# A recurrence with a feed-forward block on one core: the order of 6028 steps and the PSUM pairs of 499 rooms exchanged

## The chip, the cores and the metric

The kernel runs on one core of a Trainium2 chip. Its time is the device time in microseconds of one execution. The median of three runs of the kernel before is 1084.03 us (1081.16 to 1093.83).

## What is computed

The reference runs a state recurrence over 768 time steps for 4 batches of 8 heads, each with a 40 × 40 state, and feeds its output, as 3072 tokens of 320 numbers, to a feed-forward block with a gate:

```python
def _attn_ref(r, k, v, w, a, b):                # each (4, 8, 768, 40), float32
    ...
    for t in range(S):
        ...
        y[:, :, t] = np.einsum('bhd,bhde->bhe', rt, state)
        Sa = np.einsum('bhde,bhe->bhd', state, at)
        state_decay = state * wt[:, :, None, :] - np.einsum('bhd,bhe->bhde', Sa, bt)
        state = state_decay + np.einsum('bhd,bhe->bhde', vt, kt)
    return y

def _moe_ref(x, w_gate, w_val, w_out, rms_g):   # x (3072, 320), d_ff = 1536
    rms = np.sqrt(np.mean(x * x, axis=-1, keepdims=True) + 1e-06)
    xn = x / rms * rms_g
    g = xn @ w_gate
    silu = g * (1.0 / (1.0 + np.exp(-g)))
    val = xn @ w_val
    return silu * val @ w_out
```

The three weight matrices and the norm's gain come as given by the set-up; the matrices arrive as 64-bit floats and are narrowed to 32 bits on the chip.

## The kernel before

Time is cut into 24 chunks of 32 steps, and the recurrence inside a chunk is made into matrix products. For each chunk there are three stages, and for each two chunks a fourth:

- `front(c)` loads w, a (`wan`), k, b (`kbn`), v (`VU`) and every second w (`wn`) of the chunk, by DMAs that POOL issues (SP and ACT for chunk 0), turns them by TensorE transposes (`turned`, "turn"), and makes, by "gramk" matmuls, the products of keys with decayed a. Level by level (1, 2, 4, 8, 16 steps) DVE masks these products into the triangular matrix `LT` (`where`, a predicated copy) and forms the decayed `K`, `Ab` and `KN`; ACT copies. LT goes to DRAM (`sB`) and comes back in another layout as `M`.
- `early_inverse(c)` (chunks 0 to 3) or `inverse(c)` (the others) inverts that matrix by pairs of small DVE steps `tmp` and `Yi` (or `M`), 31 pairs for a late chunk. The result goes to DRAM (`sY`) and comes back into `LT` (or, for chunks 0 to 3, `M`) by DMAs of SP.
- `main(c)` carries the state: "state" and "lower" matmuls (`LT` with `VU`), ACT's `Xs`, a second "lower" with the inverse, a copy into `VU`, "update", a new state `ST`; then the outputs: "score" matmuls, DVE's eight masked copies `As`, one "level" matmul group for each of the five levels, and DVE's `y` steps that put them together. Then comes the norm: transposes ("turn4"), a square with sum on ACT, a `ts` on DVE, a power on POOL, a scaling on ACT, transposes ("turn3") and `xg`, the input of the feed-forward block.
- `feed(g)` (12 groups of two chunks) runs six double slices of the hidden layer: two loads `wf` from the narrowed weights `sW`, "h64" and "h" matmuls into PSUM, ACT's `sg` (SiLU), DVE's `hT`, "out" matmuls into `po`; in the end a copy `o` and the store.
- `narrow`, 24 times in the first group, loads half a slice of raw weights, makes 32-bit floats of it on ACT and DVE (`ex`), and stores it into `sW`.

None of these issues its instructions at once. `Plan.add` (L282) records each as a step with its engine and its dependences. L446 makes DVE's steps, L466, L469 and L472 ACT's, L475, L478 and L481 POOL's, L485 a DMA's issue, L488 a matmul and L491 a transpose (so nearly all rows of a profile name these helpers). A step on PE is a group of matmuls, such as the 64 of one "gramk".

`Plan.issue` (L324) then issues all 6028 steps in one written order, `ORDER` (L33 to L228), each word of which is the place of a step counted from the first step in program order that has not been issued yet. Each engine's queue is the part of this order that belongs to it, and an engine takes its queue in order: a step that waits holds up all behind it on its engine. The steps are 905 on PE, 2858 on DVE, 1024 on ACT, 545 on POOL and 696 on SP, which issues DMAs only. A word "-" stands for a filler: one 128 × 128 matmul of `ident` into an unread part of `po` (L1017). There are 151 of them.

Every PSUM result but `po` is a room: a request for one of three pairs of PSUM banks (`ps0` to `ps2`). `PAIRS` (L230 to L236) gives one digit for each of the 499 rooms, the pair that it takes. A pair holds one room at a time (`held` in `Plan.issue`): the first step that writes a room waits until the last step that reads the pair's former room is done.

The chunk and the place of a step inside its stage name it below: "front 14" is the stage `front` of chunk 14, "inverse 6" the inverse of chunk 6.

## Time and profile before

| what | us |
|---|---|
| runs: median (lowest, highest) | 1084.03 (1081.16, 1093.83) |
| span of the profiled execution | 1078.2 |
| ACT busy | 462.2 |
| POOL busy | 309.0 |

| stretch, us from the start | PE busy | DVE busy | ACT busy | POOL busy | granted PE clock |
|---|---|---|---|---|---|
| 0 to 27 | 18.09 | 20.81 | 16.70 | 25.66 | 1.00 |
| 27 to 54 | 21.60 | 22.86 | 22.07 | 19.33 | 0.75 |
| 54 to 81 | 17.66 | 21.68 | 12.64 | 4.66 | 0.79 |
| 81 to 108 | 21.45 | 19.53 | 15.56 | 11.13 | 0.83 |
| 108 to 162 | 48.40 | 41.98 | 35.28 | 14.99 | 1.00 |
| 162 to 216 | 51.88 | 48.50 | 37.01 | 18.36 | 1.00 |
| 216 to 324 | 105.73 | 78.63 | 48.15 | 31.38 | 1.00 |
| 324 to 432 | 104.59 | 92.56 | 41.18 | 29.77 | 1.00 |
| 432 to 540 | 104.01 | 87.86 | 44.97 | 32.20 | 0.98 |
| 540 to 648 | 105.38 | 93.39 | 43.64 | 35.74 | 1.00 |
| 648 to 756 | 103.92 | 89.88 | 41.82 | 27.42 | 0.98 |
| 756 to 864 | 102.12 | 86.64 | 42.15 | 32.11 | 1.00 |
| 864 to 972 | 105.41 | 92.43 | 43.49 | 25.13 | 1.00 |
| 972 to 1078.2 | 99.96 | 37.48 | 17.54 | 1.11 | 0.99 to 1.00 |

Until about 162 us the weights are narrowed and the first chunks come in, and fillers stand between PE's steps. From then on a stretch of some 82 us holds two chunks of the recurrence and one group of the feed-forward block. Some groups of the profile, with the mean time of one instruction:

```profile
L488 PE MATMUL ps<-xg,wf 128*128 128x256 f32 (+1 forms) x1728 | 355.2, 392 | 4.7 <-DVE xg L446 1.1
L488 PE MATMUL po<-wf,hT 128*128 128x320 f32 x576 | 180.1, 445 | 0.1
L446 DVE TENSOR_TENSOR tmp<-Yi,M 128x60 f32<-128x60 f32 (+24 forms) x620 | 129.5, 209 | 19.7 <-DMA M<-sB 6.9
L446 DVE TENSOR_TENSOR hT<-ps,sg 128x256 f32<-128x256 f32 x144 | 59.0, 419 | 62.4 <-ACT sg L466 55.9
L446 DVE TENSOR_TENSOR As<-ps,msi 128x256 f32<-128x256 f32 (+1 forms) x186 | 79.2, 475 | 18.3 <-PE ps L488 17.4
L488 PE MATMUL ps<-Ab,K 40*64 40x56 f32 x4608 | 88.0, 225 | 8.8 <-ACT K L469 3.7
```

A row is read thus: line, engine, operation, the tile written and the tiles read, count; behind the bar the busy time in us and the mean of one in ns; behind the second bar the idle time of the engine just before these instructions, and what ended most of it. A matmul instruction overlaps the next, so 64 of a "gramk" take 1.1 us and not 64 × 0.225.

### The profile page before, as it was taken

The numbers are of one execution on the slowest core, as the hardware profiler recorded it, in microseconds if no ns is written. First come the engines' busy times: TensorE is split into PE (matmuls) and PEld (weight loads), VectorE is DVE, ScalarE is ACT, GpSimd is POOL, SyncE is SP. The second block draws the span as 40 slices with busy tenths as digits, with TensorE's granted clock in tenths as the row PEclk, the third lists the DMA queues.
The fourth block names the chain that finished last, engine by engine and source line by source line (L and its number), as shares of the span: only waits on it lengthen the run. The fifth ranks groups of instructions, "written<-read, shape, count | busy, mean of one in ns | idle before, by whom it ended". The sixth has DMA issues, their size and how long they took to land. (4 is left out here: it accounts for less than half of the span.)

```text
span 1078.2 us, 53465 instructions
## 1 busy us (share of the span) xinstructions
PE 1010.2 (94%) x23406; PEld 828.3 (77%) x23406; DVE 834.2 (77%) x2861; ACT 462.2 (43%) x1043; POOL 309.0 (29%) x554
## 2 busy tenths in 40 slices
PE   6767899999999999999999999998999999999998
PEld 6766778777888787877788778887777887887776
DVE  7887879876868888887897888887788889797420
ACT  6845756643543433532443434433344344342211
POOL 9714404120532223241331331331332331200000
PEclk9778999999999999999999999999999999999999
DMA  9965448766564364574465654665545553744242
GB/s 180 196 155 123 73 106 220 213 127 177 124 142 122 99 150 116 144 145 120 96 152 133 146 126 112 142 142 123 126 106 110 134 150 90 162 109 123 77 140 86
DMA packets 172456, 143.34 MB, mean 133 GB/s; under 512 B 125504, under 2 KB 143872, under 8 KB 172224
## 3 DMA queue, kind: packets, MB, share of 16 engines
q1 hardware_dynamic: 153856, 116.96, 42.4%
q0 software_dynamic: 16192, 22.64, 12.2%
q8 instruction: 184, 3.01, 1.2%
q10 hardware_dynamic: 2176, 0.33, 0.2%
q14 instruction: 48, 0.39, 0.1%
HBM read 123.86 MB, written 15.99 MB: 130 GB/s over the span
## 5 line engine op out<-in xcount | busy, mean ns | idle before, releaser
L488 PE MATMUL ps<-xg,wf 128*128 128x256 f32 (+1 forms) x1728 | 355.2, 392 | 4.7 <-DVE xg L446 1.1
L488 PEld LDWEIGHTS ps<-xg,wf 128*128 128x128 f32 (+1 forms) x1728 | 261.6, 189 | 60.4 <-issue 16.9
L488 PE MATMUL po<-wf,hT 128*128 128x320 f32 x576 | 180.1, 445 | 0.1
L446 DVE TENSOR_TENSOR tmp<-Yi,M 128x60 f32<-128x60 f32 (+24 forms) x620 | 129.5, 209 | 19.7 <-DMA M<-sB 6.9
L446 DVE TENSOR_TENSOR Yi<-Yi,tmp 128x60 f32<-128x60 f32 (+24 forms) x620 | 130.2, 210 | 12.7 <-DVE ss L446 0.2
L466 ACT ACTIVATE sg<-ps 128x256 f32<-128x256 f32 x144 | 52.4, 383 | 192.4 <-PE ps L488 182.7
L488 PEld LDWEIGHTS po<-wf,hT 128*128 128x128 f32 x576 | 102.6, 191 | 34.0 <-issue 1.7
L485 POOL DMA_DIRECT2D VU<-in_v_dram x92 | 53.6, 587 | 234.2 <-PE ps L488 157.0
L446 DVE TENSOR_TENSOR hT<-ps,sg 128x256 f32<-128x256 f32 x144 | 59.0, 419 | 62.4 <-ACT sg L466 55.9
L469 ACT COPY KN<-ps 128x640 f32<-128x640 f32 x96 | 66.2, 691 | 76.6 <-PE ps L491 27.9
L488 PEld LDWEIGHTS ps<-Ab,K 40*64 40x64 f32 x4608 | 78.3, 139 | 26.4 <-issue 8.5
L446 DVE TENSOR_TENSOR K<-K,T 128x512 f32<-128x512 f32 (+1 forms) x192 | 93.3, 495 | 4.2 <-ACT K L469 2.1
L488 PE MATMUL ps<-Ab,K 40*64 40x56 f32 x4608 | 88.0, 225 | 8.8 <-ACT K L469 3.7
L485 POOL DMA_DIRECT2D kbn<-in_b_dram x92 | 53.4, 584 | 147.9 <-PE ps L488 147.0
L446 DVE TENSOR_TENSOR As<-ps,msi 128x256 f32<-128x256 f32 (+1 forms) x186 | 79.2, 475 | 18.3 <-PE ps L488 17.4
L469 ACT COPY K<-K 128x256 f32<-128x256 f32 (+1 forms) x168 | 71.8, 443 | 41.3 <-PE ps L488 20.3
L488 PEld LDWEIGHTS ps<-As,KN 128*40 128x40 f32 x3072 | 64.6, 122 | 15.1 <-issue 9.7
L485 POOL DMA_DIRECT2D wn<-in_w_dram x92 | 51.6, 565 | 83.7 <-DVE KN L446 34.7
L485 POOL DMA_DIRECT2D kbn<-in_k_dram x92 | 53.5, 585 | 73.8 <-PE ps L488 73.5
L488 PE MATMUL ps<-As,KN 128*40 128x32 f32 x3072 | 71.1, 203 | 3.7 <-issue 2.7
L446 DVE TENSOR_TENSOR y<-y,ps 128x256 f32<-128x256 f32 x119 | 49.9, 419 | 19.7 <-PE ps L488 17.6
L446 DVE COPY_PREDICATED LT<-near,ps 128x384 f32<-128x384 uint32 (+2 forms) x72 | 52.3, 727 | 3.6 <-PE ps L488 1.9
(133 smaller groups left out, 1544.5 us busy)
## 6 DMA issues: line engine op xcount, KB each, us to landing
wf<-sW SPq DMA_DIRECT2D x144, 480.0 KB, 4.3
M<-sB SPq DMA_DIRECT2D x80, 128.0 KB, 3.8
rn<-in_r_dram SPq DMA_DIRECT2D x24, 160.0 KB, 4.5
sW<-ex SPq DMA_DIRECT2D x16, 240.0 KB, 4.3
out_dram<-o SPq DMA_DIRECT2D x48, 80.0 KB, 3.9
kbn<-in_k_dram POOLq DMA_DIRECT2D x92, 40.0 KB, 3.5
kbn<-in_b_dram POOLq DMA_DIRECT2D x92, 40.0 KB, 3.3
wan<-in_a_dram POOLq DMA_DIRECT2D x46, 80.0 KB, 4.7
```

What stands on the lines that cost most here:

```text
L446: plan.add("DVE", kind, lambda at: fn(at(o), *m(at)), [o], aps(*args))
L466: plan.add("ACT", "act", lambda at: nc.scalar.activation(at(o), at(a), f, **kw), [o] + aps(acc), [a])
L469: plan.add("ACT", "copy", lambda at: nc.scalar.copy(at(o), at(a)), [o], [a])
L485: plan.add(by, "dma", lambda at: queue.dma_start(out=o, in_=i), [o], [i])
L488: return o, lhsT, rhs, lambda at: nc.tensor.matmul(at(o), lhsT, rhs, start=start, stop=stop, skip_group_check=True)
```

## The change

The two strings `ORDER` and `PAIRS` are exchanged for others. All other lines are as before; `ORDER` is 13 lines longer, so that what is L488 before is L501 after. The same 6028 steps, 151 fillers and 499 rooms are issued. Measured by its place in its own engine's queue, a step moves by up to 11 places on PE, 132 on DVE, 41 on ACT, 59 on POOL and 56 on SP; 519, 2661, 880, 507 and 645 steps have another place than before. 54 of the 499 digits of `PAIRS` differ. Between two "gramk" groups of front 2 there are 22 fillers, where there were 9.

The strings begin and end thus:

```diff
 ORDER = """
-85 84 76 83 58 78 73 86 74 59 60 75 5 89 61 88 53 77 80 4 43 6 201 7 87 90 44 8 334 62 9 - - - - - - - - 93 10 18 79
-11 12 214 557 13 213 567 14 15 94 566 210 16 17 95 558 108 200 - - - 97 96 19 335 20 21 2 209 22 23 98 25 199 568 26
...
+74 83 557 568 84 73 75 85 78 86 77 88 76 87 58 4 214 53 44 59 43 54 5 60 38 - 93 578 89 569 558 587 567 566 335 589
+577 79 586 392 48 82 334 597 2 598 94 95 6 7 8 9 10 11 12 13 14 18 15 16 17 19 108 100 20 101 - - - - - 97 - - - 23
...
 PAIRS = """
-0120112210001221022012220120200102100112221210100202110000202212201000111120112120200021220001012222000200201102100111
-0112202000011221102122212200211202022022000011000020220020011122112120010011221011122210001020022121001222220200121010
-1220202110022021220021221222111210110202012021121000002020222101010111121000120212220000221022212022101110012021110002
-0020222022211000002121122111200011110200001202211022020010021211001202102001102012021011201220022100102222202110211111
-012000001002222222210120120
+1010212220002120120222020120201101010212221210100202110000202212201000111120112120200021220001012222000200201202100111
+0112202000011221102122212200211202022022000011000220020020011122112120010011221011122220002020022121001222220200121010
+1210202102022021220021221102111210210202012121101000000022222101011111121000120212220000221212002002101110010021210002
+0020222022211000002122122111200011110200001202211022020010021212001202102001100212021011201220022000102222202110211111
+012000001202120222210012102
 """
```

On PE, one place of the queue reads like this, before and after (chunk 17, group 7 of the feed-forward block; `vut`,`rE` are the scores, `As`,`KN` the levels, `xg`,`wf` the h matmuls):

```
before   L488 score, 64 matmuls
         L488 h of one slice of group 7, 8 matmuls
         L488 level 16, level 8, level 1, level 2, level 4, 32 matmuls each
         L488 h of the other slice, 8 matmuls
after    L501 score, 64 matmuls
         L501 level 8, 32 matmuls
         L501 h of one slice of group 7, 8 matmuls
         L501 level 16, level 1, level 4, level 2, 32 matmuls each
         L501 h of the other slice, 8 matmuls
```

## The prediction

> **What bounds the kernel now.** I read the busy times first, then TensorE's waits, then the windows by stage, then single stretches.

> ```profile
> PE 1010.2 (94%) x23406; PEld 828.3 (77%) x23406; DVE 834.2 (77%) x2861; ACT 462.2 (43%) x1043; POOL 309.0 (29%) x554
> ...
> PEclk9778999999999999999999999999999999999999
> ```

> PE is busy for 1010.2 of 1078.2 us, DVE, the next, for 834.2. PE is the bound, and time is lost where PE waits. Its share of a slice is low in the first six slices only (the prologue to 162 us: 34.8 us idle in the windows), and there the granted clock is low too. From 162 us on it has 33 us idle, and this is what ended it:

> ```profile
> PE ps L488 <- issue: 12.9, 20, 1.8
> PE ps L491 <- DMA kbn<-in_k_dram: 2.1, 3, 1.1
> PE ps L491 <- DVE T L446: 1.5, 1, 1.5
> PE ps L488 <- DMA LT<-sY: 1.3, 1, 1.3
> ```

> The columns are total, times, longest. "Issue" makes 14.4 us (12.9 in this row, 1.2 and 0.3 in two others), with no cause that the trace shows; all waits for another engine's data come to 12.3 us. So the order of before feeds PE almost without a gap, and a new order is judged by the gaps that it opens.

> **The change part by part.** No operation is added or removed: 1010.2 us of PE work, 151 fillers among it, stay. Only places change: 519 of PE's 905 steps, 2661 of DVE's 2858, 880 of ACT's 1024, 507 of POOL's 545, 645 of SP's 696 stand elsewhere in their queues, by up to 11, 132, 41, 59 and 56 places; 54 of 499 PSUM pairs differ. Engines take their queues in order, so each PE step of the new order can be held against an earlier PE step (its anchor): on the one side the PE work that now stands between the two, on the other the durations of the chain from the anchor to it, through dependences, PSUM pairs coming free, and all that its DVE, ACT, POOL or SP queue now places ahead. Where the chain is longer, PE must stand still for the difference, however far the other engines have run ahead. Held over 4 us of PE work, the old order after 162 us has six such places, 3.3 us together; the trace has waits there (1.36 worked out at 360.4 us, 1.55 seen; 0.60 and 0.65 at 641.7). That check carries the rest: the new order has some 25 places. Four of them, with the prices of before's rows:

> Chunk 17, levels. These rows are PE and, last, DVE of before:

> ```profile
> 791.65 1.06 PE L488 MATMUL ps<-rE,vut 40*64 40x32 f32 x57 [0.21 <-ACT KN L469]
> 793.11 0.31 PE L488 MATMUL ps<-rE,vut 40*64 40x32 f32 x7 [0.40 <-issue]
> 793.35 1.99 PE L488 MATMUL ps<-xg,wf 128*128 128x256 f32 x8
> 795.62 1.42 PE L488 MATMUL ps<-As,KN 128*40 128x32 f32 x64 [0.27 <-DVE As L446]
> ```
> ```profile
> 793.55 3.28 DVE L446 TENSOR_TENSOR As<-ps,msi 128x256 f32<-128x256 f32 x8 [0.77 <-PE ps L488]
> ```

> Scores come first, DVE masks them into As (eight instructions, 3.28 us), the first level needs two of these, and eight feed matmuls (1.99 us) cover that: a wait of 0.27. In the new order level 8 follows the scores directly and feed's matmuls come behind it. Its own As stands behind an As (0.41), two steps of inverse 18 (0.17 each) and four As (0.68, 0.68, 0.41, 0.41), and takes 0.42 itself; as each DVE instruction starts some 0.07 before the end of the one ahead, that is 3.0 us against no PE work: +3.0. The next level there adds 1.4.

> Chunk 5, the same pattern: one gram matmul (1.12 us) between scores and level, and a DVE queue of 3.99 us (three As and five steps of gram masks, decay, K and Ab among them) before the As: +2.9.

> Chunk 12: the first lower-triangular matmul follows the gram matmuls of front 14 directly. Its PSUM pair is freed by an hT of feed 5, and in DVE's queue two predicated copies (0.72, 0.73) that need these very gram matmuls and four inverse steps (0.22 to 0.24) stand ahead of it (0.41): +2.7. In before that matmul came at 573.71 without a wait.

> Chunk 20: its last v load stands on POOL behind the power of chunk 19's norm. From the transposes: square 0.44, sum 0.15, power 0.56, one load issue 0.65, the load until landing 2.2 to 2.4; 4.23 against 1.17 of out and 0.71 of state matmuls: +2.35.

> The others, each the same subtraction: chunk 4 0.73 and 1.97, 5 1.66 (total 7.2 at 216 to 324 us with the 2.9 above); 7 0.86, 0.95, 0.31 (2.1); 10 0.62; 12 0.84 and 13 0.17 (3.7 with the 2.7); front 16 1.71, 15 0.98 (2.7); 17 0.98, 19 2.25 (7.65 at 756 to 864 with the 4.4); 20 0.36 and 2.03, 21 0.28, 1.50, 0.92 (7.4 with the 2.35); tail 2.2. The sum is 33.7 us.

> What these edits relieve: the six old places, −3.3. Of the other 9.0 us of data waits (12.3 − 3.3) new gaps nearby will take some: bounds 0 and −9.0, I take −4.5.

> The clock. PE's granted clock halves behind some waits:

> ```profile
> 498.56 0.66 PE L488 MATMUL ps<-VU,KN 64*40 64x40 f32 x45 [1.74 <-issue]
> ```
> ```profile
> 499.84:503.26 3.42, 3.42 (x33) 2.06 (x26) 2.12 (x11) 0.69 (x1) 2.52 (x5) 0.50 0.39 64
> 752.43:755.84 3.41, 3.41 (x27) 2.35 (x28) 2.49 (x10) 0.00 (x0) 0.00 (x0) 0.50 0.52 131
> ```

> A wait of 1.74, and one of 1.81 at 751.20, were followed by 3.4 us at 0.50, which cost some 1.7 us of PE time each; waits of 1.55 (360.4) and 1.31 (526.3) were not. Eight new waits exceed 1.7. Bounds 0 and 8 × 1.7 = 13.6; I take three, +5.1, since two cases on either side fix no threshold. [...]

> The prologue. Here the end of inverse 0 sets PE's start:

> ```profile
> 75.45 0.78 PE L488 MATMUL ps<-M,LT 16*16 16x16 f32 x64 [3.96 <-DMA M<-sY]
> ```
> ```profile
> 84.16 0.41 DVE L446 TENSOR_SCALAR wf<-wf 128x480 int32<-128x480 int32 x1 [7.35 <-ACT ex L466]
> ```

> In the new order 5.5 us less DVE work (59.8 to 54.3) and 6.3 us less ACT work stand ahead of inverse 0's end, and one weight-narrowing load fewer between its two sY stores on SP, so M<-sY comes earlier and the 3.96 can go. Against that, 22 fillers instead of 9 stand between two gram steps of front 2 (13 × 0.24 to 0.43 = 3 to 6 us if they are not in a gap). Ahead of 35.3 us the same subtraction finds eight short places in before, 7.9 us, and three in the new order, 3.1, some of them counted twice: up to 4.8 us. Bounds: −14 (3.96, 4.8 and the larger part of DVE's 7.35) and +3 (fillers alone); I take −6, the wait itself and half of the 4.8, rounded down.

> The v loads on POOL, in before ahead of their reader by 25 to 64 us, come just in time now in several chunks; their landing has 2.1/3.4/7.0 as minimum, median, maximum. The chain of chunk 20 used the short end; a long one adds 3.6 there, kept for the range. SP's weight loads of feed 1 now stand ahead of inverse 5's stores, and these move by 17 us to 272, still ahead of their reader: 0, but up to 3 if they land late.

> Sum: 33.7 − 3.3 − 4.5 + 5.1 − 6 = +25.0, a span of 1103.2. The median of the runs (1084.03) is 5.8 above the profiled span, so the time is 1109.

> **The rivals.** *First, the prologue opens (not slower).* Before 162 us the clock is at half in 35.6 to 49.3, 62.9 to 69.8, 76.6 to 86.8 and 100.5 to 103.9, 34.2 us which cost up to 17.1. If inverse 0's earlier end and the moved fillers keep the clock full there, −17 and the 3.96 replace the −6, and the clock term stays 0: 33.7 − 3.3 − 4.5 − 21 = +4.9, 1089; with DVE's 7.35 as well −2.5, 1081.5. For it: fillers are moved towards the gaps. Against: in that stage PE waits in many places (issue 11.7 us, ACT's K 6.7, po's first memset 3.3), most of which stay, and the half clock begins at 35.6, long before inverse 0 ends. It decides from a prologue gain of 15 on. Chance 0.11.

> *Second, the gaps overlap with "issue".* If PE's 14.4 us of issue waits are taken up in the new gaps, and no clock stretch follows: 33.7 − 3.3 − 9.0 − 14.4 − 6 = +1.0, 1085; with half of the 14.4, 1092. For it: the cause of the issue waits is not seen. Against: they lie at other places (498.6, 751.2) than the new gaps. Chance 0.10.

> *Third, worse.* All eight clock stretches and a late v load: 25.0 + 8.5 + 3.6 = +37, 1121. For it: both waits over 1.7 in the trace halved the clock. Chance 0.16.

> *Fourth, both of the first two:* 15 less than the second, 1070. Chance 0.05. My forecast keeps 0.58.

> **How the numbers follow.** The likeliest gives 1109. Without the clock term (−5.1), with all of the old waits gone (−4.5) and the prologue at −14 (−8) it is 1091; the range begins at 1090, which takes in the upper part of the second rival, and ends just over the third, at 1123. Outside lie the first, the fourth and the rest of the second, near 0.2. One per cent, about what a measurement of this kernel can tell from no change, is 10.8 us: 1073.2 and 1094.9. Faster: the fourth, 0.05. Same: the first and the second without its overlap with the forecast, 0.21 less some 0.05 for the part of either that ends above 1094.9, so 0.16. Slower: the rest, 0.79.

> **What would show it.** Right: level in chunks 5, 17 and 21 waiting 1.5 to 3 us on DVE As; lower in chunks 12 and 19 on DVE hT; in chunk 20 on the v load; PE idle between 216 and 972 us rising from 25 to about 50; DVE busy unchanged near 834; half-clock stretches behind some of those waits; PE's M<-sY wait below 2 us. Wrong: if these steps wait less than half of what is worked out, DVE's or ACT's queue is not what releases them, and the subtraction fails; if the prologue ends over 15 us earlier, the first rival holds.

## The result and the profile after

The changed kernel takes 1237.53 us (median of 4 runs, 1231.11 to 1240.39), before 1086.53 beside it: a ratio of 1.139, 95% interval 1.133 to 1.145. The forecast was 1109, its range ended at 1123. The sign was right, the size wrong by a factor of six.

Head of the page of after, busy time and granted clock:

```profile
PE 1065.3 (86%) x23406; PEld 865.3 (70%) x23406; DVE 836.9 (68%) x2861; ACT 457.8 (37%) x1043; POOL 310.9 (25%) x554
...
PEclk9767989898898998989988998989999989989999
```

DVE's work is what it was (834.2 and 836.9 us). PE differs twice: its own work takes 55.1 us longer (1010.2 to 1065.3), and it stands idle for 173.1 us (1238.4 − 1065.3) instead of 68.0. The two make the 160.2 us of the spans. The clock line has an 8 or less in 16 of 40 slices, where before had 9 from the fifth slice on: 43 us at half clock (a granted clock of 0.5) in before ((1 − 0.980) × 2 × 1078.2), 183 us in after ((1 − 0.926) × 2 × 1238.4). The loss is not in one place: PE is 4 to 11 us late at the steps around 162 us (the orders differ there), then about 60 at 400, 100 at 670 and 160 at the end.

TensorE's longest rows of waits in after from 162 us on (total, times, longest); all data waits of before there came to 12.3 us:

```profile
PE ps L501 <- DVE y L459: 19.6, 19, 2.3
PE ps L501 <- issue: 15.9, 12, 3.1
PE ps L501 <- DVE hT L459: 14.9, 11, 2.7
PE ps L501 <- DMA VU<-in_v_dram: 13.6, 5, 6.2
PE ps L501 <- DVE As L459: 8.2, 7, 3.1
```

As, hT and the v load are the releasers that were forecast; DVE's y, the largest row, is not among them. The worked places came out as forecast. Chunk 17 in after, PE's timeline:

```profile
909.68 1.28 PE L501 MATMUL ps<-As,KN 128*40 128x32 f32 x32 [3.09 <-DVE As L459]
910.90 2.95 PE L501 MATMUL ps<-xg,wf 128*128 128x256 f32 x8
...
916.22 0.81 PE L501 MATMUL ps<-As,kbn 128*40 128x32 f32 x32 [1.64 <-DVE y L459]
```

3.09 and 1.64 against 3.0 and 1.4. The eight h matmuls behind the wait take 2.95 us where before's took 1.99: the granted clock is 0.50 from 909.45 to 912.86. So the listed places are there; they are only a part of the 105 us.

### The profile page after: what moved, and what is told of

Same layout as the page of the kernel before. It is cut to its first block, busy times and chain, and to the rows that moved or that the text cites. A ratio compares the mean times of both kernels' runs of the same rounds, so it can differ in the third digit from the quotient of the medians.

```text
span 1238.4 us, 53414 instructions
## 1 busy us (share of the span) xinstructions
PE 1065.3 (86%) x23406; PEld 865.3 (70%) x23406; DVE 836.9 (68%) x2861; ACT 457.8 (37%) x1043; POOL 310.9 (25%) x554
## 4 chain that ended last, share of the span: by engine, by line
PE 51%; DVE 15%; issue 6%; DMA 6%; ACT 5%; POOL 2%; SPq 1%; DVEq 0%; ACTq 0%; POOLq 0%
PE ps L501 36%; PE po L501 8%; PE ps L504 7%; DVE y L459 2%; DMA VU<-in_v_dram 2%; DVE As L459 2%; DVE Yi L459 2%; DVE tmp L459 2%; DVE hT L459 2%; DVE LT L459 1%; SPq L498 1%; POOL kbn L498 1%; ACT sg L479 1%; DVE K L459 1%; DMA M<-sB 1%
## 5 line engine op out<-in xcount | busy, mean ns | idle before, releaser
L501 PE MATMUL ps<-xg,wf 128*128 128x256 f32 (+1 forms) x1728 | 371.6, 405 | 17.4 <-DVE hT L459 5.6
L501 PEld LDWEIGHTS ps<-xg,wf 128*128 128x128 f32 (+1 forms) x1728 | 272.0, 197 | 76.7 <-issue 14.0
L501 PE MATMUL po<-wf,hT 128*128 128x320 f32 x576 | 187.0, 458 | 8.1 <-DVE hT L459 8.0
L459 DVE TENSOR_TENSOR Yi<-Yi,tmp 128x60 f32<-128x60 f32 (+24 forms) x620 | 130.1, 210 | 13.3
L501 PEld LDWEIGHTS po<-wf,hT 128*128 128x128 f32 x576 | 106.9, 199 | 45.4 <-DVE hT L459 11.8
L501 PE MATMUL ps<-As,KN 128*40 128x32 f32 x3072 | 78.5, 211 | 36.5 <-DVE y L459 14.4
L501 PEld LDWEIGHTS ps<-As,KN 128*40 128x40 f32 x3072 | 71.0, 130 | 49.8 <-DVE y L459 17.3
L501 PEld LDWEIGHTS ps<-Ab,K 40*64 40x64 f32 x4608 | 81.5, 146 | 27.1 <-issue 11.1
L501 PE MATMUL ps<-Ab,K 40*64 40x56 f32 x4608 | 90.3, 232 | 10.6 <-DVE K L459 7.9
L482 ACT COPY K<-K 128x256 f32<-128x256 f32 (+1 forms) x168 | 73.4, 444 | 34.8 <-PE ps L501 24.3
L1030 PE MATMUL po<-ident 128*128 128x128 f32 x302 | 56.0, 327 | 3.3 <-DVE po L532 3.3
```

What stands on the lines that cost most here:

```text
L459: plan.add("DVE", kind, lambda at: fn(at(o), *m(at)), [o], aps(*args))
L482: plan.add("ACT", "copy", lambda at: nc.scalar.copy(at(o), at(a)), [o], [a])
L501: return o, lhsT, rhs, lambda at: nc.tensor.matmul(at(o), lhsT, rhs, start=start, stop=stop, skip_group_check=True)
L1030: plan.warm = lambda: nc.tensor.matmul(po_[:, 0, DM:DM + P], ident, ident, start=False, stop=False, skip_group_check=True)
```

## The experiments

The kernels below differ from before or after in `ORDER` and `PAIRS` alone. A ratio is to the runs of before on the same chip.

**e1: before's queues, another interleaving.** `ORDER` is one list for five engines. In e1 every engine keeps before's queue; what changes is where words of ACT and DVE stand between those of PE. In 51 of the 72 double slices, 17 more than in before, the SiLU of the first half stands behind the other half's h, and the words behind these SiLUs in their queues move along (104 words in all, by 1 to 6 words of PE). For instance in group 11:

```diff
  PE  feed 11, h of the first half
  PE  feed 11, out
- ACT feed 11, SiLU of the first half
  PE  feed 11, h of the second half
+ ACT feed 11, SiLU of the first half
```

> Before's five queues and PAIRS, word for word the same order on each engine; only the interleaving of the engines in ORDER differs: in 51 of the 72 double slices of the feed-forward block (34 in before) the first half's SiLU on ACT is now issued behind the second half's h matmuls. Theory W: what an instruction waits for is fixed by the order of issue over all engines, and for a PSUM pair as a whole, so that such a SiLU waits for the other half's matmuls too; ACT's queue, DVE's hT and PE then run late. Slower by 35 to 75 us (1120 to 1160), with ACT's sg waiting longer on PE and PE on DVE hT. Rival Q (my prediction's assumption): only queue order and true dependences count, so the same as before within 1% (1075 to 1097).

1126.94 us, ratio 1.042 (1.037 to 1.048). Theory W holds and rival Q falls: nothing on any engine's queue has moved, and the kernel loses 43 us. They belong to the 104 words together, as the 17 SiLUs cannot be moved alone. The groups of ACT's SiLU and DVE's hT, before and then e1 (busy, mean ns, then the idle time ahead and what ended it), show the way it takes:

```profile
L446 DVE TENSOR_TENSOR hT<-ps,sg 128x256 f32<-128x256 f32 x144 | 59.0, 419 | 62.4 <-ACT sg L466 55.9 <-PE ps L488 5.5
L466 ACT ACTIVATE sg<-ps 128x256 f32<-128x256 f32 x144 | 52.4, 383 | 192.4 <-PE ps L488 182.7 <-DVE hT L446 4.7 <-DVE Yi L446 3.5
```
```profile
L445 DVE TENSOR_TENSOR hT<-ps,sg 128x256 f32<-128x256 f32 x144 | 59.1, 419 | 105.0 <-ACT sg L465 104.1
L465 ACT ACTIVATE sg<-ps 128x256 f32<-128x256 f32 x144 | 51.9, 383 | 230.7 <-PE ps L487 227.3 <-DVE hT L445 3.3
```

ACT waits 45 us more for PE before its SiLUs, and DVE 48 us more for ACT before hT. PE's issue waits are as in before (25 and 26 us).

**e2: after's queues, another interleaving.** The counterpart: after's five queues and pairs, with all words of `ORDER` put in the order in which the steps could start by their true dependences, for instance

```diff
  PE  feed 9, h of the half that comes first
+ ACT feed 9, SiLU of that half
  PE  feed 9, h of the other half
- ACT feed 9, SiLU of the first half
```

> After's five queues and PAIRS; only the interleaving of the engines in ORDER is made anew (every step issued in the order in which it could start by its true dependences). SiLUs issued behind the other half's h: 30 instead of 42. Theory W: a good part of what after loses over the predicted 25 us comes back: 40 to 85 us less than after (1150 to 1197), the rest stays, since the queues themselves are after's. Rival Q: no change (1225 to 1250). Rival C (all beyond the forecast is the clock, queues alone decide the waits): no change either.

1194.13 us, ratio 1.103 (1.097 to 1.110): 43 us less than after (38 by the two ratios) with every queue the same, at the small end of the 40 to 85 that W expected. PE's waits for SiLU and hT fall from 30.7 us (5.5, 14.9, 8.0 and 2.3 in four rows) to 13.3 (0.8, 5.8, 3.4 and 3.3); before has 1.1. But 3793 words of the other engines have another place among PE's than in after, so not all of the gain need come from SiLUs. This one SiLU in after, PE first, then ACT:

```profile
1072.78 3.06 PE L501 MATMUL ps<-xg,wf 64*128 64x256 f32 x16
...
1078.65 1.89 PE L501 MATMUL ps<-xg,wf 128*128 128x256 f32 x8
1083.89 1.39 PE L501 MATMUL ps<-Ab,K 40*64 40x56 f32 x41 [3.35 <-DVE K L459]
```
```profile
1080.58 0.38 ACT L479 ACTIVATE sg<-ps 128x256 f32<-128x256 f32 x1 [5.77 <-PE ps L501]
```

and in e2, where PE runs the same steps in the same order:

```profile
1027.18 3.06 PE L500 MATMUL ps<-xg,wf 64*128 64x256 f32 x16
...
1033.05 1.89 PE L500 MATMUL ps<-xg,wf 128*128 128x256 f32 x8
1034.87 1.16 PE L500 MATMUL ps<-Ab,K 40*64 40x56 f32 x64
```
```profile
1030.27 0.38 ACT L478 ACTIVATE sg<-ps 128x256 f32<-128x256 f32 x1 [1.07 <-PE ps L500]
```

The first row of PE ends with the h matmuls of the first half (the 16 are h64 and these). In e2 the SiLU starts 0.03 us after them (1030.24). In after its own data are there at 1075.84, but it starts at 1080.58, just when the other half's h (1078.65 and 1.89) has ended. ACT has stood for 5.77 us; DVE waits 3.16 us for a copy that ACT makes behind the SiLU, and the next gram matmul of PE, which has no wait in e2, waits 3.35 for DVE. In after this SiLU is issued behind the other half's h, in e2 ahead of it, and both halves are in the same PSUM pair. No run here tells a bank from the whole pair.

**e3: the clock.** Fillers in the place of waits: 327 words "-" ahead of matmul groups of after that wait 0.5 us or longer.

```diff
+ - - - - - - - - - -        (as many as fit in 0.8 of the wait)
  PE main 17, level 8
```

> After with 327 fillers more on PE, put ahead of the 80 or so matmul groups after 100 us that wait 0.5 us or longer in after, as many as fit in 0.8 of the wait at 0.24 us each: 78 us of matmuls in the place of idle time. If the half clock is a consequence of these waits (PE's low share in a window of 3.4 us, whatever the longest single wait), the half-clock time falls from 182 us to under 90, and the time by 30 to 65 us (1172 to 1207), though PE does more work. If the half clock does not come from them, or if the waits alone cost the time, it is the same or slower by up to 20 us (1225 to 1260).

1232.55 us, ratio 1.138 (1.132 to 1.144), the same as after: the clock went as the theory had it, the time did not. Half clock falls from 183 to 86 us, so a good half of it came from the waits that were filled. PE's other matmuls take 968.5 us instead of 1009.3 (PE busy less the fillers' 146.8 and 56.0), 40.8 less. But the fillers cost 90.8 us more and the idle time falls by 65.2 only, which takes back 25.6 of the 40.8. The other 15.2 are the difference of the two profiled spans (after's is the longest of its four runs, e3's the shortest; the medians differ by 5). PE's issue waits grew as well, from 19 to 34 us; more fillers also shift PE's stream (e9 to e11 below). How much of the 55 us the clock alone costs is not settled by this run.

**e4: the prologue alone.** After's order up to the step at 162 us, before's from there.

```diff
- before's steps and pairs up to the step at 162 us
+ after's steps and pairs up to that step
  before's steps and pairs from there on
```

> After's order up to the step that starts at 162 us in before, before's order and pairs from there on. At the end of that stage after's trace is 4 us behind before's at the same step. Theory: the prologue carries next to nothing of the result, 1080 to 1096, the same within 1%. Rival (the prologue leaves buffers and loads out of step and the whole run pays for it): over 1120. My forecast of the prologue (-6): 1078 to 1082.

1088.01 us, ratio 1.004 (1.001 to 1.008). The prologue carries at most 0.8% of the 13.9%; my forecast for it, 1078 to 1082, falls.

**e5 and e6: the listed places, and as many steps elsewhere.** Both are e2 with before's relative order of the steps in some stretches of `ORDER`: e5 in those that hold the 25 places (1651 steps), e6 between them (1663 steps).

```diff
- PE score (chunk 17), level 8, h, level 16, ...       after's order, e6
+ PE score (chunk 17), h, level 16, level 8, ...       before's order, e5
```

> After, with before's relative order (on all engines) in 14 stretches of ORDER that hold the 25 places of the prediction's list, 1651 of 6028 steps in all; 2 stretches are some 300 steps, most about 100. Interleaving made anew by the same rule as e2, so e2 (1194) is what it is held against. Theory L: the listed places are where the new queues cost, so that a quarter of the steps takes back most of what is left: 1194 minus 34 for the listed waits and minus 15 to 25 for the clock and for late SiLUs inside these stretches, 1130 to 1150. Rival S (the loss is spread over all moved steps): a quarter of e2's loss, some 28 us, 1160 to 1172.

> The counterpart of e5: before's relative order in 12 stretches that lie between the 25 places and hold none of them, 1663 steps; interleaving by the same rule. Theory L: no more than 1% from e2, 1182 to 1204. Rival S: as e5, 1160 to 1172.

e5: 1147.27, ratio 1.062 (1.057 to 1.068). e6: 1184.27, ratio 1.095 (1.087 to 1.102). Theory L holds: the same number of steps is worth 4.1% where the subtraction found places and 0.9% where it did not (e6's interval overlaps e2's). (PE's issue waits are 16 us in e5 and 25 in e6, so some 9 us of the 37 between them are not the places'.)

**e7: the v loads.** 85 of POOL's v loads issued earlier in after.

```diff
+ POOL front 20, v load        (60 words behind the last reader of its buffer)
  ...
  POOL main 19, power
- POOL front 20, v load
```

> After, with 85 of POOL's 92 v loads issued earlier, 60 words of ORDER behind the last step that their buffer waits for; nothing else moved. In after PE waits 13.6 us in 5 places for v (up to 6.2), where the prediction had 2.4 and 6 at the most. Theory: these waits go, and with them up to 3 stretches of half clock (1.7 us each): 1219 to 1228. Rival (other chains end just behind them): 1232 to 1242. Other side: POOL's queue is held up by loads that wait for their buffers, over 1245.

1224.04, ratio 1.134 (1.127 to 1.140) against after's 1.139. PE's row of waits for v loads, 13.6 us in after, is gone from the trace. The median is 13.5 us below after's, but before was 9 us faster beside it too: by the ratios the gain is 0.5%, some 6 us, and the two intervals overlap, so the size is not measured.

**e8: before with a filled prologue.** 33 fillers more in four waits before 80 us.

```diff
+ - - - - - - - - - - - -
  PE inverse 0, first matmuls
```

> Before, with 33 fillers more ahead of four matmul groups that wait 1.8 to 4.0 us before 80 us. Half clock before 110 us is 34 us in before; if fillers keep it full and PE's steps there are on the path of inverse 0, up to 10 us less (1073 to 1082); if DVE, ACT and the loads set the prologue, the same within 1% (1078 to 1092).

1127.51, ratio 1.043 (1.036 to 1.050): neither. PE was 4 us ahead of before at 162 us, and lost 52 us after it, in an order that had not been touched. Waits of PE over the whole span, before and then e8:

```profile
PE ps L488 <- issue: 21.9, 29, 1.9
```
```profile
PE ps L488 <- issue: 52.7, 42, 4.8
```

**e9, e10, e11: the place in PE's stream.** e9 is e8 with 33 later fillers taken out, so that from 235 us on as many instructions of PE stand ahead of each step as in before; e10 and e11 are before with 7 and 16 fillers more at the start.

```diff
+ - - - - - - -               (e10)
  PE front 0, first transposes
```

> e8 (33 fillers more before 80 us, 1127 against 1078) with 33 of before's own fillers taken out between 174 and 235 us, so that from 235 us on PE's stream has as many instructions ahead of each step as in before. In e8 PE was 4 us ahead at 162 us and lost 52 us after it, with no other order changed; its issue waits were 53.4 us (26 in before) and in the trace of every kernel these lie at multiples of 127 matmuls of PE's stream. Theory F (issue waits are waits for blocks of PE's own instructions, and the shift by 33 moved the blocks' ends to other steps): the loss goes, 1074 to 1090, issue waits 20 to 35. Rival (the fillers in the prologue put something else out of step): 1110 to 1130.

> Before with 7 fillers more ahead of the first step, where PE waits for loads until 6.8 us, so that all blocks of PE's stream end 7 matmuls earlier in the work, and nothing else differs. Theory F: issue waits anywhere between 15 and 55 us and the time with them, 1072 to 1130, by more than 1% off before as likely as not. Rival (the stream's place does not matter): 1074 to 1086, issue waits 26 as in before.

> As e10 with 16 fillers more (7 ahead of the first step, 5 and 4 in waits up to 33 us). Theory F: another sum of issue waits than in before and e10, 15 to 55 us, 1072 to 1130. Rival: 1074 to 1088, issue waits 26.

e9: 1086.25, ratio 1.005 (1.002 to 1.009). e10: 1115.78, ratio 1.032 (1.025 to 1.039). e11: ratio 1.045 (1.037 to 1.053). Theory F's range for e10 and e11 was wide, but its rivals fall. The seven fillers of e10 do not all fit in idle time: the first transposes begin at 9.25 us instead of 6.85. Of that nothing is left at inverse 0 (74.75 us instead of 75.45), and still the kernel loses 3%. Its issue waits are 37 us instead of 26, its half clock is 91 us instead of 43, and PE's work takes 21 us longer. The largest row of e10, to be held against the 21.9 us of before:

```profile
PE ps L488 <- issue: 30.8, 35, 2.6
```

And e9 shows that e8's loss goes with the shift, not with its fillers.

**e12 and e13: what is left, and a better version.** e12 is after with before's prologue, e5's stretches, earlier v loads and e2's interleaving; e13 is before with e8's fillers and 33 of its own taken out between 102 and 175 us.

```diff
+ before's order to 162 us, e5's stretches, 64 v loads early     (e12)
+ e8's 33 fillers before 80 us; 33 fewer at 102 to 175 us        (e13)
```

> After with four repairs at once: before's order up to the step at 162 us, before's relative order in e5's 14 stretches, 64 v loads on POOL issued earlier as in e7, and the interleaving of e2. The rest, three quarters of the steps after 162 us, keeps after's order. Theory: the parts add, e5's 1147 less 13 (v loads) less 6 (prologue, e5 is 7.5 us behind before at 162 us): 1120 to 1135; the 40 to 55 us over before that are left belong to the other moved steps, with late SiLUs among them. Rival (the parts are one chain, and with these gone the rest is hidden): under 1105.

> Before with e8's 33 fillers more before 80 us, and 33 of before's own taken out between 102 and 175 us: PE's stream has before's place again from 175 us on, earlier than in e9 (235), which gained 6.4 us up to 162 us and lost them again where its fillers were missing at 171 to 200. Theory F: issue waits as in before; 1071 to 1080, up to 1% faster. Rival (the fillers at 102 to 135 us are needed too): 1080 to 1092.

e12: 1133.40, ratio 1.053 (1.046 to 1.059), inside the theory's range: 5% are left, and PE's issue waits (24 us) are no longer than before's. By the ratios the repairs added to e5 are worth 1.0%, some 10 of the 19 us expected, and the intervals overlap. e13: 1083.25, ratio 1.006 (1.002 to 1.009): no better than before. Theory F's 1071 to 1080 falls, though the issue waits are only 21 us; the half clock is 72 us instead of 43, and why is open. No version here beats before.

## Why the prediction was wrong

**The step that failed** is the one that everything rested on: "Engines take their queues in order, so each PE step of the new order can be held against an earlier PE step": on the chain's side it counted dependences, PSUM pairs coming free and what is ahead in the own queue. It left out that a SiLU here also waits for the matmuls that PE had been given on its PSUM pair before it in `ORDER`, whether it needs them or not (5.77 us for the one shown under e2, 1.07 where it stands ahead of them). I compared the five queues and never the interleaving. e1 shows that this alone can cost 43 us with all queues unchanged, e2 that 43 us of after's 151 hang on the interleaving. That the subtraction agreed with before's waits said little: there 34 of the 72 double slices have such a late SiLU too (42 in after), but PE has other work meanwhile and waits only 1.1 us for SiLU and hT (30.7 in after). This step is not the whole miss of 128 us: the clock term below and places that are not on the list have their parts, which overlap with it and were not separated.

**The 33.7 us of the list** were right in place and a little small: the listed steps wait about 46 us in after. Chunk 12 was worked out at 2.7 and waits 2.65, chunk 5 2.9 and 3.15, chunk 17 3.0 and 3.09, chunk 19 2.25 and 2.12. The largest miss is chunk 20:

```profile
1018.01 1.28 PE L501 MATMUL ps<-VU,LT 32*32 32x40 f32 x62 [6.24 <-DMA VU<-in_v_dram]
```

6.24 against 2.35. The load was issued at 1012.02 (as worked out, behind the power at 1010.71) and the matmul began at 1018.01, 6.0 us later. I had taken the short end of the landing times for the sum and kept the long one, 3.6 us more, for the range; it was the long one. e5 and e6 confirm that the list finds costly places. But PE's idle time from 162 us on went from 33 to 138 us, where the list alone would have added 34: most places where after waits are not on it.

**The relief of old waits** (−3.3, −4.5) does not show: the data waits from 162 us on grew from 12.3 to 115 us.

**The clock term** was put at 5.1 us with 13.6 as its bound, and PE's work grew by 55. That the clock halves behind waits was right: half clock fell from 183 to 86 us where e3 filled them. The size failed at "Eight new waits exceed 1.7": I counted long single waits of my own list, but the clock went with the idle time in a window of 3.41 us (half clock behind 13 of 13 windows of after with 2.0 us or more of it, the last section has the counts), short waits add up in it (1.70 and 0.36 us in the window at 165.3), and most of the new idle time (105 us, of which the list has about 46) was not on the list.

**The prologue** was put at −6. In the trace PE is 2 to 3 us ahead at 80 us, as the M<-sY wait did get shorter (2.2 us in two waits), but 4 to 11 us late at 162 us: other waits took its place. e4 bounds what it carries at 0.8%.

**Rivals.** The second had the 14.4 us of issue waits from 162 us on taken up by new gaps. After's rows there say 16.7, but three of these waits (2.65, 2.12 and 3.07, at the "lower" matmuls of chunks 12, 19 and 21) end 0.10 us behind an hT on DVE and are waits for it. The other 8.9 are 5.5 less than before's, so this rival was right in part, and nothing against the new waits. The third, "worse", named the right things, clock and a late v load, but the 12 us that it adds to the forecast are a tenth of the 128 that were missing.

**Not settled:** the 5% of e12, which that run leaves with the other three quarters of the moved steps. Late waits of the same kind that no interleaving of after's queues removes (in e2 30 SiLUs still stand behind the other half's h) and places with chains longer than the 4 us that I looked at are both possible; neither was separated. Nor is the part of the clock in the 151 us.

## What to carry to other kernels

When an order of issue is exchanged, compare the order across engines and not only each engine's queue: here a SiLU issued behind an unrelated h on its PSUM pair waited for it (5.77 us in after, 1.07 in e2, where it is issued ahead), and its word could be moved ahead without a change to any queue. A subtraction of chain against cover from one trace found costly places of the new order here, several of them to a few tenths of a us, but its sum was far too low, since most waits were not on its list and TensorE's clock halved behind waits (183 us at half clock in after, 86 in e3). Before a small difference between two kernels is explained, look whether the same instructions of TensorE stand at the same place in its stream: seven fillers more at the start cost 3.2% in e10.

## What the hardware showed that was not expected

**Blocks of PE's instructions.** The page of before counts PE's own instructions as a DMA queue:

```profile
q8 instruction: 184, 3.01, 1.2%
```

184 packets of 16 KB for 23406 matmuls and as many weight loads are 127 matmuls a packet; e3, with 654 matmuls more, has 189. The waits put down to "issue" lie on a grid of 127.1 matmuls (in before at matmuls 1486, 1614 and 1741; in e8 at 14327, 14960 and 15721): all 31 of before that are 0.2 us or longer to within 5 matmuls, all 42 of e8 to within 3. In before, 28 of the 31 follow a block of 127 that took 4.8 us or less, as blocks of small matmuls do; of the 152 boundaries without a wait 54 do. The longest is in e8:

```profile
173.43 0.39 PE L488 MATMUL ps<-M,LT 16*16 16x16 f32 x29 [4.75 <-issue]
```

A filler is two matmuls in the trace, so 7 to 33 fillers shift the stream by 14 to 66. That moves the boundaries to other work, and issue waits went from 26 us to 53 in e8 and 37 in e10, and the half clock from 43 us to 88 and 91.

```profile
906.04:909.45 3.41, 0.56 (x40) 0.45 (x32) 3.38 (x10) 0.00 (x0) 1.33 (x3) 1.00 0.55 108
909.45:912.86 3.41, 3.18 (x37) 2.76 (x38) 0.84 (x3) 0.00 (x0) 0.00 (x0) 0.50 0.81 241
```
